# A hand-written order for the first four chunks of a recurrent-attention and two-MLP kernel

## Chip, core and metric

The kernel runs on one core of a Trainium2 chip. The metric is the device time of one execution in microseconds (us); below, the time is that of the profiled execution or the median of several, as said. Engines are named as in the profile: PE (TensorE, matmuls), PEld (its weight loads), DVE (VectorE), ACT (ScalarE), POOL (GpSimd), SP (SyncE, whose queue issues all DMAs here).

## What is computed

A recurrent state update per batch and head, whose output goes through a dense MLP, whose output goes through a layer of eight weighted experts:

```
B, H, S, D = 4, 8, 768, 40
for t in range(S):
    y[:, :, t] = einsum('bhd,bhde->bhe', r_t, state)
    Sa = einsum('bhde,bhe->bhd', state, a_t)
    state = state * w_t[:, :, None, :] - einsum('bhd,bhe->bhde', Sa, b_t) + einsum('bhd,bhe->bhde', v_t, k_t)
x = y as (3072, 320)
h = x @ w_in                                  # 320 x 2048
x = where(h > 0, h, exp(min(h, 0)) - 1) @ w_out
P = exp(x @ w_gate - max); 8 times: rows and columns normalised
out = sum over 8 experts e of P[:, e:e+1] * (relu(x @ w1[e]) @ w2[e])
```

`w_in` and `w_out` arrive as 64-bit floats.

## The kernel before

**Recurrence.** The 768 steps are cut into 24 chunks of 32. `loadw`, `loadk`, `loadv` and `loads2` load a chunk's w and a (`WA`), k and b (`KE`), v (`VU`) and r. `prep` (L308) makes the running products with two scans on DVE (`F` L318, `xE` L324), scales a (`aE`) and copies it to `aB`, and scales `KE` on POOL. `E3` multiplies a against k and b and masks the product on DVE into `Am`; the lower half goes through DRAM (`Ad`), and `LT` loads it back in the layout of the triangular solve. `tsolve` (L401) solves one or two chunks: 31 steps of a product (L416) and a difference (L423) on DVE, and then stores (`Td`) and loads (`TT`) through DRAM. From here the chunks are serial: `H1`, `H2` (needs `TT`, matmuls L462), `H3` and `YW` carry the state from chunk to chunk; `O1` to `O3b` make the chunk's output.

**First MLP.** A block is 256 tokens, two chunks; 12 blocks. `xprep` turns a block's output into `X`. A block is 16 units, one for each 128 columns of `w_in`: eight matmuls L587 into `ph`, two ACT instructions `m`, `g` on DVE (L596), a split into `gh` (ACT) and `gl` (POOL), and two units later eight matmuls L614 to L618. Fp32 products are made from split halves.

**Conversion.** `w_in` and `w_out` stand in SBUF as split fp32, in 32 tiles (16 each). A tile is a load into `raw` (two buffers), an absolute value on ACT (L196), four integer instructions on DVE (L197 to L200, `to_f32`), one copy on ACT and two differences on POOL. A unit n needs the tiles of `w_in` up to n and of `w_out` up to n-2 (`ready`).

**Second MLP.** `phase_b`: per expert, block of 512 tokens and 128 columns, eight matmuls L772, `hh` (ACT), `hl` (DVE), and twelve matmuls L812 to L814.

**What sets the order.** `PLAN["start"]` is a list of tokens for chunks 0 and 1, all conversion (`w_n`: n tiles) and some of chunks 2 to 5. From chunk 2, `PLAN["order"]` is run once for each chunk c: a token `n+o` advances step n of chunk c+o, `m` advances the first MLP by half a unit, `p` advances the solve (three instructions), `G` lets the solve begin, `x` and `xl` advance `xprep`. The scheduler places the instructions of the start and of chunks 2 and 3 by its own model, moved by `issue_after` and `high_priority`. From chunk 4 (`"fixed": 4`) `pin_since` ties every instruction of DVE, ACT, POOL and PE to the one before it in the program, so that the engines run in the written order; SP is not tied. In chunks 2 to 4 only three of four `m` count (`acc`):

```
acc += 3 if c < 5 else 4
if acc >= 4:
    next(mg)
    acc -= 4
```

Of the kernel before, what the change touches and what calls it, by code (L numbers as in the profile page):

```python
# [30 lines left out]
    "fixed": 4,  # L31
    "eng": {"RH": "AA", "VU": "AAAA", "YW": "G", "SS": "AA", "UE": "AV", "XT": "A", "KB": "AA", "AB": "AA"},
# [66 lines left out]
def build(ctx, tc, r, k, v, w, a, b, w_in, w_out, wg, w1, w2, wa_d, kb_d, re_d, ro_d, vt_d, wp_d, consts, out, C, off):  # L99
# [14 lines left out]
    PINNED = {x.engine for x in (V, A, G, T)}  # L114
# [77 lines left out]
    dve = {}  # L192

    def to_f32(raw, tmp):
        lo, hi, m = raw[:, :, 0], raw[:, :, 1], tmp.bitcast(I32)
        A.activation(out=tmp, in_=hi.bitcast(F32), func=AF.Abs)  # L196
# [3 lines left out]
        dve["w"] = V.scalar_tensor_tensor(out=m, in0=lo, scalar=29, in1=m, op0=ALU.logical_shift_right, op1=ALU.bitwise_or)  # L200
        return tmp

    def conv_tiles(n):
        raw = cv.tile([128, n * e32], I32 if wide else F32, tag="raw", name="raw").rearrange("p (f e) -> p f e", e=e32)
        return raw, cv.tile([128, n], F32, tag="tmp", name="tmp", bufs=2) if wide else None

    def w_in_split(cx, n):
        raw, tmp = conv_tiles(3 * n)
        raw = raw.rearrange("p (k f) e -> p k f e", k=3)
        SY.dma_start(out=raw.rearrange("p k f e -> p (k f e)"), in_=wp_d[cx])  # L210
        rf = raw.rearrange("p k f e -> p (k f) e")
        x = (to_f32(rf, tmp) if wide else rf[:, :, 0]).rearrange("p (k f) -> p k f", k=3)
        dl = slice(cx * n, (cx + 1) * n)
        A.activation(out=Wt[:, 0:3, dl], in_=x, func=AF.Copy)
        G.tensor_tensor(out=Wt[:, 3:5, dl], in0=x[:, 0:2, :], in1=Wt[:, 0:2, dl].bitcast(F32), op=ALU.subtract)
        G.tensor_tensor(out=Wt[64:128, 2, dl], in0=x[64:128, 2, :], in1=Wt[64:128, 2, dl].bitcast(F32), op=ALU.subtract)

    def w_out_split(f):
        raw, tmp = conv_tiles(DM)
        SY.dma_start(out=raw.rearrange("p f e -> p (f e)"), in_=wo_d[f * 128:(f + 1) * 128, :])  # L220
        x = to_f32(raw, tmp) if wide else raw[:, :, 0]
        A.activation(out=Wo(f)[:, 0:320], in_=x, func=AF.Copy)
        G.tensor_tensor(out=Wo(f)[:, 320:384], in0=x[:, 256:320], in1=Wo(f)[:, 256:320].bitcast(F32), op=ALU.subtract)
# [84 lines left out]
    def prep(c):  # L308
# [17 lines left out]
        G.tensor_tensor(out=z.aE[0:HR].rearrange("p g t -> p (g t)"), in0=z.WA[0:HR, 1].rearrange("p g t -> p (g t)"), in1=flat(z.xE)[0:HR], op=ALU.mult)  # L326
# [74 lines left out]
    def tsolve(*cs):  # L401
        n = len(cs)
        x0 = cs[0] % 3
        LT2 = LTs[:, x0:x0 + n] if x0 + n <= 3 else LTs[:, ::-2]
        Wk = WkT
        tmp = r1.tile([128, 2 * CI * (C - 1)], F32, tag="Tt", name="Tt")
        w0 = 0 if n == 2 else cs[0] % 2
        Wk = Wk[:, w0:w0 + n]
        SY.dma_start(out=Wk.rearrange("p x i t -> p x (i t)"), in_=consts[:, nidk:nidk + CI * C].unsqueeze(1).to_broadcast([128, n, CI * C]))
        yield  # L410
        for j in range(C - 1):
# [97 lines left out]
    def O1(c):  # L509
# [499 lines left out]
    with ExitStack():  # L1009
        loads(0)  # L1010
# [20 lines left out]
        def ready(n):  # L1031
# [3 lines left out]
            if not wgen:  # L1035
                return True
# [25 lines left out]
        def step(n, c):  # L1062
            if 0 <= c < NCH and (n, c) not in done:
                po = PLAN["po"].get(n, 0)
                with tc.high_priority(offset=po) if po else ExitStack():
                    run_all(fns[n](c) or ())
                done.add((n, c))

# [11 lines left out]
        def solve(n):  # L1080
            for _ in range(n):
                if pump and next(pump[0], "end") == "end":
                    pump.pop(0)
                    pumping.pop()

        def conv(n):
            for _ in range(n):
                if wgen:
                    fn, *ar = wgen.pop(0)
                    cvd.add(("i" if fn is w_in_split else "o", ar[0]))  # L1090
                    with tc.issue_after(dve["A"].ins) if "A" in dve else ExitStack():
                        fn(*ar)
                    if not wgen:
                        cvx.close()
                        late.append(moe.enter_context(tc.tile_pool(name="late", bufs=1)))

        order = [(t.split("+")[0], int((t + "+0").split("+")[1])) for t in PLAN["order"].split()]
        with ExitStack():
            rec_init()
            for t in PLAN["start"].split():  # L1100
                n, *cs = t.split("_")
                cs = [int(x) for x in cs]
                if n == "w":
                    conv(*cs)
                elif n == "xl":
                    xgen.append(xprep(0))
                    run_all(xgen.pop())
                    ms["xp"] = 1
                elif n == "T":
                    with tc.issue_after(dve["w"].ins) if "w" in dve else ExitStack():  # L1110
                        run_all(tsolve(*cs))
                    dve["A"] = dve["T"]
                    done.update(("T", x) for x in cs)
                elif n == "u":
                    advance("T", cs[0])
                elif n == "t":
                    with tc.high_priority(offset=PLAN["po"]["T"]):
# [74 lines left out]
```

## Time and profile before

| What | us |
|---|---|
| median of three runs (2338.56 to 2345.97) | 2342.83 |
| the profiled execution's own time | 2343.14 |
| its span | 2341.0 |
| PE busy in it | 2169.7 |
| DVE busy | 988.0 |
| ACT busy | 752.7 |
| POOL busy | 472.2 |

The span is the time between the first and the last recorded instruction; 2.1 us of the execution lie outside it. Busy times of the engines overlap one another. A line such as "251.35 0.28 PE L462 MATMUL P<-RH,TT ... x2 [1.25 <-DMA TT<-Td]" reads: at 251.35 us from the start, 0.28 us long, line 462 of the kernel, output and inputs by the program's names, two instructions, and the engine had been idle for 1.25 us until a DMA into TT from Td landed.

### The profile page before, as it was taken

Reading aid. Unit: us, or ns where it says so; the run is one execution under the profiler, and the core shown is the slowest. Engines: PE = TensorE matmul, PEld = TensorE weight load, DVE = VectorE, ACT = ScalarE, POOL = GpSimd, SP = SyncE. Lnnn points to the kernel's source line nnn. Section 1 sums busy time; section 2 is a strip of 40 time slices with the busy share of each in tenths; the row PEclk is TensorE's granted clock in tenths of the full one; section 3 lists DMA queues with packets and bytes.
Section 4 is the critical chain, followed back from the end, with each engine's and each line's share of the span. In section 5 each row is a group of like instructions: output and inputs, shape, how many; then the busy total and the mean of one; then the engine's idle time right before and its main releaser. Section 6 shows DMA issues by size and latency. Waiting matters only on the chain.

```text
span 2341.0 us, 47093 instructions
## 1 busy us (share of the span) xinstructions
PE 2169.7 (93%) x19908; PEld 1968.5 (84%) x19908; DVE 988.0 (42%) x2112; ACT 752.7 (32%) x1663; POOL 472.2 (20%) x556
## 2 busy tenths in 40 slices
PE   2377899999999999999999999999999999999998
PEld 2266788888888998888988988988988988988887
DVE  6788666677777522532222222222222222222222
ACT  3243354555555556323212112112112112112111
POOL 5254244343343226002002002002002002001000
PEclk9987799999999999999999999999999999999999
DMA  5344333343333223101001001001001001000000
GB/s 158 99 141 112 92 94 97 102 108 96 100 91 101 64 57 104 60 1 41 10 1 45 6 1 45 6 1 45 6 1 47 4 1 47 4 1 20 23 23 25
DMA packets 171589, 121.62 MB, mean 52 GB/s; under 512 B 102825, under 2 KB 151337, under 8 KB 171369
## 3 DMA queue, kind: packets, MB, share of 16 engines
q1 hardware_dynamic: 171368, 118.52, 18.8%
q8 instruction: 158, 2.59, 0.5%
q14 instruction: 63, 0.51, 0.1%
HBM read 99.99 MB, written 18.48 MB: 51 GB/s over the span
## 4 chain that ended last, share of the span: by engine, by line
PE 73%; DVE 11%; DMA 8%; SPq 3%; ACT 2%; issue 2%; POOL 1%; DVEq 0%; ACTq 0%; POOLq 0%
PE h L772 30%; PE pa L812 9%; PE pa L813 9%; PE pa L814 9%; PE ph L587 4%; DVE Wk L423 3%; DVE Tt L416 2%; DMA LT<-Ad 2%; PE a L614 2%; DMA WA<-in_wa 1%; DMA Ad<-Am 1%; PE a L616 1%; PE a L615 1%; DMA raw<-in_wp 1%; PE P L544 1%
## 5 line engine op out<-in xcount | busy, mean ns | idle before, releaser
L772 PE MATMUL h<-X,a 128*128 128x512 f32 x3072 | 782.0, 396 | 0.6 <-DVE X L575 0.6
L772 PEld LDWEIGHTS h<-X,a 128*128 128x128 f32 x3072 | 564.1, 188 | 107.4 <-DVE X L575 0.8
L776 DVE SCALAR_TENSOR_TENSOR hl<-h,hh 128x512 fp32r<-128x512 f32 x384 | 264.9, 690 | 884.1 <-ACT hh L775 884.0
L775 ACT ACTIVATE hh<-h 128x512 fp32r<-128x512 f32 x384 | 229.3, 598 | 1030.5 <-PE h L772 1022.6
L813 PE MATMUL pa<-a,hl 128*128 128x320 f32 x1536 | 475.1, 310 | 0.0
L812 PE MATMUL pa<-a,hh 128*128 128x320 f32 x1536 | 473.7, 310 | 0.3 <-ACT logits L642 0.3
L814 PE MATMUL pa<-a,hh 128*128 128x320 f32 x1536 | 469.3, 310 | 0.0
L813 PEld LDWEIGHTS pa<-a,hl 128*128 128x128 f32 x1536 | 289.3, 188 | 17.9
L812 PEld LDWEIGHTS pa<-a,hh 128*128 128x128 f32 x1536 | 289.8, 189 | 15.3 <-ACT logits L642 0.4
L814 PEld LDWEIGHTS pa<-a,hh 128*128 128x128 f32 x1536 | 287.4, 188 | 0.0
L740 POOL TENSOR_TENSOR a<-rw,a 128x384 fp32r<-128x384 f32 x64 | 65.2, 1018 | 1062.9 <-ACT a L738 1059.5
L600 POOL TENSOR_TENSOR gl<-g,gh 128x256 fp32r<-128x256 f32 x192 | 165.0, 859 | 396.3 <-ACT gh L598 305.5
L587 PE MATMUL ph<-X,Wt 128*128 128x256 f32 x1536 | 237.3, 299 | 6.1 <-DVE g L596 6.1
L587 PEld LDWEIGHTS ph<-X,Wt 128*128 128x128 f32 x1536 | 206.3, 199 | 11.3 <-DVE g L596 7.3
L423 DVE TENSOR_TENSOR Wk<-Wk,Tt 128x120 f32<-128x120 f32 (+30 forms) x403 | 158.1, 392 | 9.3 <-DVE Tt L416 0.2
L596 DVE SCALAR_TENSOR_TENSOR g<-m,ph 128x256 f32<-128x256 f32 x192 | 80.0, 417 | 167.4 <-ACT m L590 143.3
L416 DVE TENSOR_TENSOR Tt<-Wk,LT 128x120 f32<-128x120 f32 (+30 forms) x403 | 130.8, 324 | 37.0 <-DMA LT<-Ad 12.9
L823 DVE SCALAR_TENSOR_TENSOR acc<-pa,Pg,acc 128x320 f32<-128x320 f32 x168 | 84.3, 544 | 116.0 <-PE pa L814 116.0
L598 ACT ACTIVATE gh<-g 128x256 fp32r<-128x256 f32 x192 | 80.0, 417 | 144.5 <-DVE g L596 143.5
L589 ACT ACTIVATE m<-ph 128x256 f32<-128x256 f32 x192 | 73.2, 381 | 142.2 <-PE ph L587 135.0
L590 ACT ACTIVATE m<-m 128x256 f32<-128x256 f32 x192 | 80.0, 417 | 5.7
L614 PE MATMUL a<-gh,WoB 128*128 128x256 f32 x216 | 71.0, 329 | 1.2 <-ACT gh L598 1.2
(168 smaller groups left out, 2295.7 us busy)
## 6 DMA issues: line engine op xcount, KB each, us to landing
LT<-Ad SPq DMA_DIRECT2D x24, 512.0 KB
rw<-in_moe_w SPq DMA_DIRECT2D x64, 160.0 KB
WA<-in_wa SPq DMA_DIRECT2D x24, 416.0 KB
KE<-in_kb SPq DMA_DIRECT2D x24, 416.0 KB
rw<-in_moe_w SPq DMA_DIRECT2D x64, 128.0 KB
VU<-in_vt SPq DMA_DIRECT2D x24, 320.0 KB
raw<-in_wp SPq DMA_DIRECT2D x16, 384.0 KB
raw<-in_moe_w_out SPq DMA_DIRECT2D x16, 320.0 KB
```

What stands on the lines that cost most here:

```text
L416: V.tensor_tensor(out=tv, in0=Wk[:, :, 0:ni, j:j + 1].to_broadcast(sh), in1=LT2[:, :, j, j + 1:C].unsqueeze(2).to_broadcast(sh), op=ALU.mult,)
L423: dve["T"] = V.tensor_tensor(out=Wk[:, :, 0:ni, j + 1:C], in0=Wk[:, :, 0:ni, j + 1:C], in1=tv, op=ALU.subtract)
L587: T.matmul(ph, lhsT=Wt[0:kp, wi, 128 * f:128 * f + 128], rhs=X[0:kp, xi, :], start=(i == 0), stop=(i == 7))
L600: G.tensor_tensor(out=gl, in0=g, in1=gh.bitcast(F32), op=ALU.subtract)
L614: T.matmul(o, lhsT=Wo(f)[:, 128 * i:128 * i + 128], rhs=gh, start=(s and i == 0), stop=False, skip_group_check=True)
L772: T.matmul(h, lhsT=a1[:, wi, :], rhs=X[bk][:, xi, :], start=(i == 0), stop=(i == 7))
L775: A.activation(out=hh, in_=h, func=AF.Relu)
L776: V.scalar_tensor_tensor(out=hl, in0=h, scalar=0.0, in1=hh.bitcast(F32), op0=ALU.max, op1=ALU.subtract)
L812: T.matmul(o, lhsT=hh[:, ts_], rhs=a2[:, 0, :], start=(f == 0), stop=False)
L813: T.matmul(o, lhsT=hl[:, ts_], rhs=a2[:, 0, :], start=False, stop=False)
L814: T.matmul(o, lhsT=hh[:, ts_], rhs=a2[:, 1, :], start=False, stop=(f == NF2 - 1))
L823: V.scalar_tensor_tensor(out=at, in0=o, scalar=Pg[:, tt, e:e + 1], in1=at, op0=ALU.mult, op1=ALU.add)
```

## The change

The four parts of it, cut to their core (the steps themselves are those above):

- The start and the lists of chunks 2 and 3 (`"first"`) are written out and pinned on all engines and on SP's queue. `prep_0*5` stands for five tokens, `s_n` for n steps of a solve. In chunks 2 and 3 every `m` counts.
- Conversion goes one tile per `p`, 4 tiles' steps in the start (`w`) and the rest in chunks 2 and 3; the steps of neighbouring tiles are staggered (`conv`).
- Chunks 2 and 3 are solved as one pair, with their factors in the memory of chunk 1's `WA` and `KE` (`two`) and their unknowns in that of chunk 1's `wq`.
- Solve 4/5 follows the conversion, 16 instructions per `p`. `aE` of chunks 0 and 1 is made on DVE, `E1` of chunks 0 and 1 uses other PSUM banks, and `uE` of chunks below 4 is copied on ACT.

```diff
-    PINNED = {x.engine for x in (V, A, G, T)}
+    PINNED = {x.engine for x in (V, A, G, T, SY)}
-            if x.engine in PINNED:
+            if x.engine in PINNED and (queue or x.engine != SY.engine):
...
+        def conv_begin():
+            convs.extend(conv_load(*wlist[i]) for i in range(2))
+            conv_abs(convs[0])
...
+        def conv():
+            k = cvn[0]
+            if k > NW:
+                return False
+            if k:
+                conv_out(convs[k - 1])
+            if k + 1 < NW:
+                conv_abs(convs[k + 1])
+            if k < NW:
+                conv_bits(convs[k])
+            if k + 2 < NW:
+                convs.append(conv_load(*wlist[k + 2]))
...
+    def lt(c):
+        return two[:, c - 2].rearrange("p (s t) -> p s t", s=C) if c in (2, 3) else LTs[:, c % 3]
...
+        LT2 = two.rearrange("p x (s t) -> p x s t", s=C) if cs[0] == 2 else LTs[:, x0:x0 + n] if x0 + n <= 3 else LTs[:, ::-2]
+        Wk = work[1][1].rearrange("p (x i) t -> p x i t", x=2) if cs[0] == 2 else WkT
...
-                if n == "w":
-                    conv(PLAN["wn"])
-                elif n == "m":
-                    acc += 3 if c < 5 else 4
-                    if acc >= 4:
-                        next(mg)
-                        acc -= 4
+                if n == "m":
+                    next(mg)
                 elif n == "p":
-                    if pumping:
-                        pk += 1
-                        solve(PLAN["tp"][c % 2][pk % 2])
+                    if c >= 4 or not conv():
+                        if pumping:
+                            solve(PLAN["tp"][c % 2] if c >= 4 else PLAN["tp1"])
...
-                if c >= PLAN["fixed"]:
-                    pin_since(last)
+                pin_since(last, c < 4)
```

What it does to the order is seen in three places. First DVE while the second solve runs: before, the single solve of chunk 2 (`Tt`, `Wk`) alternates with the four conversion instructions of a tile (`tmp`).

```order
L200 SCALAR_TENSOR_TENSOR tmp<-raw,tmp 128x320
L416 TENSOR_TENSOR Tt<-Wk,LT 128x69
L423 TENSOR_TENSOR Wk<-Wk,Tt 128x3x23
L197 TENSOR_SCALAR tmp<-tmp 128x384
L416 TENSOR_TENSOR Tt<-Wk,LT 128x66
L198 TENSOR_SCALAR tmp<-tmp 128x384
L423 TENSOR_TENSOR Wk<-Wk,Tt 128x3x22
L199 SCALAR_TENSOR_TENSOR tmp<-raw,tmp 128x384
```

With the change, DVE at the end of chunk 3: the last tile's four instructions, a unit's `g`, the output of chunk 3 (`xT`), and only then solve 4/5.

```order
L200 TENSOR_SCALAR tmp<-tmp 128x320
L201 TENSOR_SCALAR tmp<-tmp 128x320
L202 SCALAR_TENSOR_TENSOR tmp<-raw,tmp 128x320
L203 SCALAR_TENSOR_TENSOR tmp<-raw,tmp 128x320
L625 SCALAR_TENSOR_TENSOR g<-m,ph 128x256
L576 TENSOR_TENSOR xT<-P_101,xT 128x160
L576 TENSOR_TENSOR xT<-P_102,xT 128x160
L444 TENSOR_TENSOR Tt<-Wk,LT 128x62
L451 TENSOR_TENSOR Wk<-Wk,Tt 128x2x31
L444 TENSOR_TENSOR Tt<-Wk,LT 128x60
```

No tile of the conversion is left behind this place, and no solve stands between the tiles of chunks 2 and 3. Second, SP's queue with the change, where solve 2/3 ends (`Td` from `wq`): the stores and loads of both chunks come in a row, and the next `raw` load waits behind them.

```order
L218 DMA raw<-in_moe_w_out 128x640
L456 DMA Td<-wq_143 256x1x32 x8
L462 DMA TT_109<-Td 32x8x32 x4
L462 DMA TT_110<-Td 32x8x32 x4
L218 DMA raw<-in_wp 128x768
L437 DMA Wk<-in_consts 128x2x256
L331 DMA rB<-in_re 40x8x64 x2
L333 DMA rO<-in_ro 104x512
L218 DMA raw<-in_moe_w_out 128x640
L218 DMA raw<-in_wp 128x768
```

Before, the two chunks are solved apart, and single `raw` loads stand between the stores and loads of each. Third, PE around `H2` of chunk 6 (L491 with the change): from the last unit ahead of it to the next, no matmul of the first MLP stands here.

```order
L429 MATMUL P_99<-VU,Am_116 64x40 x8
L429 MATMUL P_100<-VU,Am_116 64x40 x8
L393 MATMUL P_102<-aB,KE 64x64 x16
L479 MATMUL P_99<-Yw,aE 32x40 x16
L479 MATMUL P_100<-Yw,aE 32x40 x16
L384 MATMUL P_101<-cst,xE 128x104 x4
L491 MATMUL P_100<-RH,TT_109 64x40 x16
L375 MATMUL P_101<-cst,KE 128x104 x4
L375 MATMUL P_102<-cst,KE 128x104 x4
L599 MATMUL P_102<-cst,yt 128x128 x3
L514 MATMUL P_99<-VU,KB 40x40 x16
```

Before, each of these steps has a half of a unit beside it. Counted on PE ahead of `H2` of chunks 4, 5, 6 and 7, there are 14, 20, 28 and 36 units (L587) before, and 18, 26, 32 and 36 (L616) with the change; from chunk 7 on the two orders of PE agree.

## Rows read from the trace of the kernel before

**Rows 1.** Windows: us, busy per engine (with counts), granted PE clock, DMA share, GB/s.
```profile
93.80:162.00 68.20, 47.19 (x713) 39.49 (x713) 56.49 (x157) 30.02 (x69) 30.13 (x44) 0.96 0.48 141
162.00:251.30 89.30, 67.27 (x933) 59.09 (x929) 72.58 (x183) 31.54 (x81) 36.23 (x41) 0.68 0.41 105
251.30:350.80 99.50, 89.32 (x1518) 83.44 (x1518) 68.54 (x158) 50.42 (x126) 36.18 (x42) 0.93 0.39 99
...
417.70:871.50 453.80, 426.30 (x7369) 399.04 (x7368) 289.01 (x683) 243.37 (x617) 166.11 (x197) 0.98 0.35 89
871.50:2341.00 1469.50, 1455.72 (x8144) 1312.57 (x8140) 393.66 (x695) 333.91 (x626) 140.61 (x157) 1.00 0.08 23
```

**Rows 2.** Timeline of PE: `H2` of chunks 0, 1, 4, 5, 6, 7.
```profile
88.99 0.41 PE L462 MATMUL P<-RH,TT 64*64 64x40 f32 x2 [18.28 <-DMA TT<-Td]
...
113.42 2.00 PE L462 MATMUL P<-RH,TT 64*64 64x40 f32 x32 [0.50 <-ACT RH L438]
...
251.35 0.28 PE L462 MATMUL P<-RH,TT 64*64 64x40 f32 x2 [1.25 <-DMA TT<-Td]
...
285.80 1.13 PE L462 MATMUL P<-RH,TT 64*64 64x40 f32 x32
316.91 1.13 PE L462 MATMUL P<-RH,TT 64*64 64x40 f32 x32
350.78 1.13 PE L462 MATMUL P<-RH,TT 64*64 64x40 f32 x32
```

**Rows 3.** Timeline of DVE: first and last step of solves 0/1 and 4/5.
```profile
51.72 0.16 DVE L416 TENSOR_TENSOR Tt<-Wk,LT 128x62 f32<-128x62 f32 x1
...
81.78 0.18 DVE L423 TENSOR_TENSOR Wk<-Wk,Tt 128x16 f32<-128x16 f32 x1
...
219.68 0.22 DVE L416 TENSOR_TENSOR Tt<-Wk,LT 128x62 f32<-128x62 f32 x1 [6.33 <-DMA Ad<-Am]
...
242.85 0.18 DVE L423 TENSOR_TENSOR Wk<-Wk,Tt 128x16 f32<-128x16 f32 x1
```

**Rows 4.** The chain that ended last, in order of time: start, us, what.
```profile
42.40 7.18 DMA WA<-in_wa
...
452.32 3.86 DMA Ad<-Am
456.19 4.56 DMA LT<-Ad
```

**Rows 5.** Timeline of ACT: absolute values of tiles 1, 8 and 27 of 32.
```profile
13.33 0.55 ACT L196 ACTIVATE tmp<-raw 128x384 f32<-128x384 f32 x1 [1.22 <-DMA raw<-in_wp]
...
93.85 0.56 ACT L196 ACTIVATE tmp<-raw 128x384 f32<-128x384 f32 x1
...
162.01 0.48 ACT L196 ACTIVATE tmp<-raw 128x320 f32<-128x320 f32 x1
```

**Rows 6.** Groups by line: a tile's four DVE instructions; busy us, mean ns, idle before.
```profile
L199 DVE SCALAR_TENSOR_TENSOR tmp<-raw,tmp 128x384 int32<-128x384 int32 (+1 forms) x32 | 20.3, 638 | 0.2
...
L200 DVE SCALAR_TENSOR_TENSOR tmp<-raw,tmp 128x384 int32<-128x384 int32 (+1 forms) x32 | 19.3, 604 | 0.2
...
L197 DVE TENSOR_SCALAR tmp<-tmp 128x384 f32<-128x384 f32 (+1 forms) x32 | 15.2, 478 | 14.5 <-ACT tmp L196 14.4
...
L198 DVE TENSOR_SCALAR tmp<-tmp 128x384 int32<-128x384 int32 (+1 forms) x32 | 14.3, 449 | 0.3
```

**Rows 7.** Timeline of DVE: one step of solve 0/1 beside a product on POOL.
```profile
60.27 0.30 DVE L423 TENSOR_TENSOR Wk<-Wk,Tt 128x132 f32<-128x132 f32 x1
60.60 1.15 DVE L416 TENSOR_TENSOR Tt<-Wk,LT 128x126 f32<-128x126 f32 x1
```

**Rows 8.** Timeline of POOL at that time.
```profile
60.36 2.42 POOL L335 TENSOR_TENSOR KE<-KE,F 104x512 f32<-104x512 f32 x2 [2.43 <-DMA KE<-in_kb]
```

**Rows 9.** Timeline of PE: the first half of a unit, twice.
```profile
144.44 2.07 PE L587 MATMUL ph<-X,Wt 128*128 128x256 f32 x8
...
340.09 1.22 PE L587 MATMUL ph<-X,Wt 128*128 128x256 f32 x8
```

More of the change, by code (lines that the diff above doesn't have):

```diff
@@ L118, in traced, with pin_since @@
         return nc.cur_bb.bb.instructions
-    def pin_since(last):
+    def pin_since(last, queue):
         ins = traced()
-        k = next(k for k in reversed(range(len(ins))) if ins[k] is last) + 1
+        k = next(k for k in reversed(range(len(ins))) if ins[k] is last) + 1 if last is not None else 0
         for x in ins[k:]:
-            if x.engine in PINNED:
+            if x.engine in PINNED and (queue or x.engine != SY.engine):
                 if x.engine in pins:
@@ new lines, in to_f32, with conv_load @@
+    def to_f32(raw, tmp):
+        f32_abs(raw, tmp)
+        f32_bits(raw, tmp)
+        return tmp
+    convs = []
+    cvd = set()
+    def conv_load(kind, i):
+        z = K()
+        z.kind, z.i = kind, i
+        n = 384 if kind == "i" else DM
+        z.raw = cv.tile([128, n * e32], I32 if wide else F32, tag="raw", name="raw")
+        SY.dma_start(out=z.raw, in_=wp_d[i] if kind == "i" else wo_d[i * 128:(i + 1) * 128, :])
+        z.rv = z.raw.rearrange("p (f e) -> p f e", e=e32)
+        z.n = n
+        return z
@@ new lines, in conv_abs, with conv_bits, conv_out @@
+    def conv_abs(z):
+        if wide:
+            z.x = cv.tile([128, z.n], F32, tag="tmp", name="tmp")
+            f32_abs(z.rv, z.x)
+        else:
+            z.x = z.rv[:, :, 0]
+    def conv_bits(z):
+        if wide:
+            f32_bits(z.rv, z.x)
+    def conv_out(z):
+        if z.kind == "i":
+            x = z.x.rearrange("p (k f) -> p k f", k=3)
+            dl = slice(z.i * 128, z.i * 128 + 128)
+            A.activation(out=Wt[:, 0:3, dl], in_=x, func=AF.Copy)
+            G.tensor_tensor(out=Wt[:, 3:5, dl], in0=x[:, 0:2, :], in1=Wt[:, 0:2, dl].bitcast(F32), op=ALU.subtract)
+            G.tensor_tensor(out=Wt[64:128, 2, dl], in0=x[64:128, 2, :], in1=Wt[64:128, 2, dl].bitcast(F32), op=ALU.subtract)
+        else:
+            f, x = z.i, z.x
+            A.activation(out=Wo(f)[:, 0:320], in_=x, func=AF.Copy)
+            G.tensor_tensor(out=Wo(f)[:, 320:384], in0=x[:, 256:320], in1=Wo(f)[:, 256:320].bitcast(F32), op=ALU.subtract)
+            G.tensor_tensor(out=Wo(f)[:, 384:640], in0=x[:, 0:256], in1=Wo(f)[:, 0:256].bitcast(F32), op=ALU.subtract)
+        cvd.add((z.kind, z.i))
@@ L255, in build @@
     work = {None: (wr, wq, dq, aB)}
+    two = sp.tile([128, 2, C * C], F32, name="two")
     def rec_init():
@@ L265, in rec_init @@
             V.memset(bank[i], 0.0)
-        for t in (aB, wmm, rB, *TTs, Yw):
+        work[1] = (early(1, "wr", [4 * NG, C + 1]), early(1, "wq", [4 * NG, C]), early(1, "dq", [4 * NG, C]), early(1, "aB", [NG * 2 * 2, 64]).rearrange("p (g u j) t -> p g u j t", u=2, j=2))
+        for t in (aB, wmm, *work[1]):
             G.memset(t, 0.0)
@@ L269, in rec_init, with rec_init2 @@
         G.memset(whalf, 1e-5 - (WHI - WLO) / 2)
+    def rec_init2():
         for i in (0, 1):
             V.memset(bank[i], 0.0)
+        for t in (rB, *TTs, Yw):
+            G.memset(t, 0.0)
     def flat(t):
@@ L1009, in build @@
     with ExitStack():
+        first_ins = traced()[-1] if traced() else None
         loads(0)
@@ L1051, in build @@
         mg = msteps()
-        cvd = set()
-        wi_ = [(w_in_split, i, 128) for i in range(NF1)]
-        wo_ = [(w_out_split, i) for i in range(NF1)]
         k0 = PLAN["lead"]
-        wgen = wi_[:k0]
+        wlist = [("i", i) for i in range(k0)]
         for i in range(NF1):
-            wgen += wi_[k0 + i:k0 + i + 1] + wo_[i:i + 1]
+            wlist += [("i", k0 + i)] * (k0 + i < NF1) + [("o", i)]
+        NW = len(wlist)
         fns = dict(ld=loads, ldw=loadw, ldk=loadk, lu=loadv, lv=loads2, prep=prep, H1=H1, H2=H2, H3=H3, H4=H4, E1=E1, E2=E2, E3=E3, E4=E4, T=tsolve, O1=O1, O2=O2, O3a=O3a, O3b=O3b, YW=YW, LT=LT)
         done = {("ld", 0), ("ld", 1)}
[L1062 to L1067, printed above, removed]
         going = {}
@@ L1083, in solve @@
                     pump.pop(0)
[L1084 to L1102, printed above, removed]
-                if n == "w":
[L1104 to L1117, printed above, removed]
-                        run_all(going[("T", cs[0])])
-                    done.add(("T", cs[0]))
-                else:
-                    step(n, cs[0])
@@ L1122, in build @@
-        acc = pk = 0
+                    if pumping:
+                        pumping.pop()
+        def conv_begin():
+            convs.extend(conv_load(*wlist[i]) for i in range(2))
+            conv_abs(convs[0])
+        cvn = [0]
+        def conv():
[10 more added lines that the diff above has]
+                convs.append(conv_load(*wlist[k + 2]))
+            if k == NW:
+                cvx.close()
+                late.append(moe.enter_context(tc.tile_pool(name="late", bufs=1)))
+            cvn[0] += 1
+            return True
@@ new lines, in tokens @@
+        def tokens(x):
+            out = []
+            for t in x.split():
+                t, k = (t + "*1").split("*")[:2]
+                out += [t] * int(k)
+            return out
+        rec_init()
+        pin_since(first_ins, True)
+        for t in tokens(PLAN["start"]):
+            last = traced()[-1]
+            n, *cs = t.split("_")
+            cs = [int(x) for x in cs]
+            if n == "cl":
+                conv_begin()
+            elif n == "w":
+                conv()
+            elif n == "z":
+                rec_init2()
+            elif n == "xl":
+                xgen.append(xprep(0))
+                run_all(xgen.pop())
+                ms["xp"] = 1
+            elif n == "u":
+                pump.append(tsolve(*(cs if len(cs) == 2 else (cs[0], cs[0] + 1))))
+                next(pump[-1])
+            elif n == "s":
+                had = len(pump)
+                for _ in range(cs[0]):
+                    if len(pump) == had:
+                        solve(1)
+            else:
+                advance(n, cs[0])
+            pin_since(last, True)
@@ L1123, in build @@
+        acc = 0
         for c in range(2, NCH + 1):
-            for n, o in order:
+            for t in tokens(PLAN["first"][c - 2] if c < 4 else PLAN["order"]):
+                n, o = (t.split("+") + ["0"])[:2]
+                o = int(o)
                 last = traced()[-1]
-                if n == "w":
-                    conv(PLAN["wn"])
-                elif n == "m":
-                    acc += 3 if c < 5 else 4
-                    if acc >= 4:
-                        next(mg)
-                        acc -= 4
+                if n == "m":
+                    next(mg)
@@ L1143, in build @@
                     if c % 2 == 0 and c + 3 < NCH:
+                        while pump:
+                            solve(1)
                         pump.append(tsolve(c + 2, c + 3))
```

68 lines of the change are left out of this document (24 added, 44 removed), and 10 rows, old and new, of the table PLAN.

## Prediction

> **What bounds the kernel now.** I first read the windows [rows 1]. From 871.5 us to the end PE is busy 1455.7 of 1469.5 us: the second MLP is bound by PE, and the change does not touch it. From 417.7 to 871.5, the chunks in their fixed order, PE is busy 94%. From 93.8 to 251.3 it is busy 114.5 of 157.5 us, at a granted clock that falls to 0.68 in the second part. What can be won lies there and ahead of it, where PE waits for the recurrence and the conversion. DVE has the most work in that part: 56.5 of 68.2 us, 83%, from 93.8 to 162.
>
> Next I looked for a mark behind which both programs are the same. That is `H2` of chunk 7 [rows 2]: at 350.78 us, and by the order both programs have put 36 units of the first MLP on PE ahead of it, and the same sequence behind it. So the time with the change is 2343.1 us, the profiled execution's own (0.3 above the median of the runs), less what this mark moves forward. The six units by which the change is ahead at chunk 5 (26 against 20) are no gain by themselves: block 2 needs the output of chunk 5, so the lead is used up in chunk 6, where the order shows no units. What stays is only the mark's place in time.
>
> **The parts of the change, in order of time.**
>
> *Up to the first solve.* Before, solve 0/1 begins at 51.72 [rows 3], behind five tiles of conversion and four preparations. With the change only three preparations and two tiles precede it, and ACT's queue begins with the first tile's absolute value, which has its data at 13.33 [rows 5]; the copies of `aB` stand behind it, about 15 us. WA of chunk 2 goes into chunk 0's buffer, whose last reader is ACT, at about 17; such a load takes 7.2 [rows 4], the preparation and the mask product some 3, and `Ad` and `LT` 3.9 + 4.6 [rows 4]. 17 + 7.2 + 3 + 8.4 = 35.6: I take 36. Bounds: 30, if the load takes half of it, and 52, if nothing is won.
>
> *Solve 0/1.* Before it takes 30.2 us (51.72 to 81.96) with two waits for WA; solve 4/5, with less beside it, takes 23.3 (219.68 to 243.03) [rows 3]. Between them, as one preparation and two mask products lie inside: 28, so it ends at 64.
>
> *Chunks 0 and 1.* From the end of solve 0/1 to `H2` of chunk 0 it was 7.0 us (81.96 to 88.99) [rows 2, 3]: 71. From there the order binds solve 2/3 to the serial chain of both chunks: DVE has no other work, and can't run ahead of the waits for `Y`, `Gm` and `xT`. Before, `H2` of chunk 1 came 24.4 us behind that of chunk 0 [rows 2], with conversion in between on DVE. A chain of two chunks without it I put at 35 (an estimate: the 24.4 cut to 15 as the tiles go, and 20 for chunk 1 with its output and `xprep`); bounds 30 and 49 (twice 24.4). The end is 106, where the first unit can start.
>
> *Into the conversion.* The sixth tile's load stands on SP behind the 16 stores and loads of solve 2/3, which cost DVE and ACT a wait. From the end of a solve to `H2` behind these DMAs it was 7.0 and 8.3 us (243.03 to 251.35) [rows 2, 3]; then its own load, ACT, four instructions of 2.2 us in all [rows 6], and the seventh tile the same: 18, so the seventh tile leaves DVE at 124. Bounds 12 and 22.
>
> *The tiles.* 25 more tiles follow, each with its share of four preparations, two chunks and 15 units. Before, with the same two buffers, the absolute values of tiles 8 and 27 are 68.2 us apart, 19 steps: **3.59 us a tile** [rows 5]. The loop is the load into a buffer, ACT, DVE, and the load again. I take 3.59: 90 us, to 214. The lower bound is DVE at work all the time: 56.5 us in that stretch for 19 tiles is 2.97. Before, a solve stood between the tiles; now it is preparations and units, about as much. The upper bound comes with the rivals.
>
> *Solve 4/5* now follows the tiles, beside few units: 23.3, to 237. *`H2` of chunk 4* comes 8.3 later [rows 2, 3]: 245.4, against 251.35 before. So the hand-written order wins only 6 us here: the 16 us of the early start are mostly given back, as 28 of 32 tiles and a whole solve now stand in a row behind chunk 1.
>
> *Chunks 4 to 6.* Before, 99.4 us from there to the mark, with 22 units. Now 18 units. A half of a unit is 1.22 us at full clock [rows 9], a whole one 2.44, four of them 9.8. It counts in full where PE is the bound: before, chunk 5 to 6 takes 31.1 us with 8 units [rows 2], and PE is busy 89.3 of 99.5 in the stretch [rows 1]. Chunk 6 will in part be bound by its chain instead; I take 9 (bounds 0 and 14, with the slower clock at its start won as well): 90.4, to 335.8.
>
> The mark moves from 350.8 to 335.8, and the sum is 2343.1 - 15.0 = **2328 us**. With a cadence of c us a tile it is 2328 + 25 (c - 3.59).
>
> What I cost at nothing: `aE` of two chunks on DVE instead of POOL, which DVE hides in its wait for WA; the clearing of banks moved behind the first preparation, in the same wait; other PSUM banks for `E1`; the copy of `uE` on ACT. If DVE does not wait there, they cost about 3 us. SP, now tied too, has in chunks 2 and 3 a wait for `Ad` ahead of each `LT`, with tiles' loads behind it: up to 3.9 us [rows 4], three times, and I count it in the 3.59, in whose stretch of the trace such waits fall as well.
>
> A rule and a row. A step of the solve that takes 0.30 us takes 1.15 while POOL multiplies in SBUF [rows 7, 8]. The Trainium skill, page "SBUF — State Buffer", section "Who interferes with whom", says that a DVE instruction with two SBUF inputs contends with a GpSimd instruction that reads SBUF, and that the later one blocks until the other is done; the trace agrees with it (0.30 against 1.15 us). By this rule the change is to lose, since it puts the differences of a tile on POOL and the next tile's two-input instructions on DVE at the same time, unit after unit; that is the second rival.
>
> **The rivals.**
>
> *DVE sets the pace of the tiles* (chance 0.23). If the staggered steps hide load and ACT, c is 2.97 and the time 2328 - 15.5 = 2312. For it: each absolute value is issued a whole tile ahead. Against it: with two buffers a load can't start before DVE has left the buffer.
>
> *POOL blocks DVE* (0.18). If each tile loses one half of a blocked step, 0.43 us, DVE's work is 3.40 a tile, and at the 83% of before c is 4.10: 2341, no change. For it: POOL was busy 30.1 of 68.2 us [rows 1] and now has units all along. Against: the 3.59 and the means of rows 6 hold some of this already.
>
> *PE stays at half clock through chunks 2 and 3* (0.10), the slower side. Half a unit took 2.07 us at 144 against 1.22 at 340 [rows 9], though the profile gives a clock of 1.0 for the early part, and between 162 and 251 the clock was 0.68 with PE busy 75% [rows 1]. The lower level is 1.2 GHz. At it a unit is 4.1 us, and a chunk's other matmuls (31.1 less eight units is 11.6 at full clock) up to 23, 2.9 a unit: 7.0 a unit, 3.5 a tile if PE never waits, 4.7 at 75%. That gives 2356, slower; the point from which it decides is a cadence of 4.5. The Trainium skill, page "TensorE: Matmul & The Clock Gate", Part 1, says that the throttled state is the default and that activity releases it; no run here shows yet how these two chunks will fare.
>
> *The early start does not come* (0.05): the queue is now bound, and a late load holds all behind it. With the first solve at 52 the time is 2344, the same as before.
>
> **How the numbers follow.** The forecast, a cadence near 3.6, has 0.42, and by itself 2318 to 2338. About 0.3% (7 us) is what a measurement of this kernel can tell from no change. Faster: most of 0.42, all of 0.23 and a little of the second rival, 0.62. Same: 0.25. Slower: 0.13, the third rival and the bounds that add up (a chain of 49 instead of 35). The range for 8 in 10 reaches from 2304, the first rival with the early bounds, to 2350, past the second rival and short of the third.
>
> **What would show it.** In the profile of the changed kernel: the first solve step at 33 to 40 us; `H2` of chunk 0 near 71; the first unit near 106; 25 tiles at 3.3 to 3.9 us; solve 4/5 alone for 23 us, beginning near 214; `H2` of chunk 4 near 245 and of chunk 7 near 336; no units around `H2` of chunk 6; and from the mark to the end of the span the 1990 us of before (2341.0 - 350.8). I am wrong if the distance from the mark to the end differs by more than 5 us, if the cadence lies outside 3.2 to 4.2, or if PE is the engine that the tiles wait for.

## The result and the profile after

The changed kernel takes 2360.35 us (median of four runs, 2353.38 to 2363.02) against 2340.69 for the kernel before beside it: ratio 1.0076, 95% interval 1.0052 to 1.0100. It is slower, by 0.8%; I had forecast 2328, with 2350 as the upper end. The profiled execution takes 2363.02 us, with a span of 2361.2.

Windows of the changed kernel, cut at the points of the forecast (columns as in [rows 1]): `H2` of chunk 0, the seventh tile leaving DVE, the last tile leaving DVE, `H2` of chunks 4 and 7, the end.

```profile
0.00:74.18 74.18, 17.68 (x208) 15.25 (x209) 59.65 (x129) 18.89 (x39) 22.57 (x32) 0.68 0.55 146
74.18:124.23 50.05, 29.12 (x660) 25.89 (x662) 36.20 (x77) 15.96 (x37) 14.82 (x19) 0.64 0.27 65
124.23:236.60 112.37, 70.96 (x871) 66.04 (x869) 83.65 (x139) 53.22 (x127) 50.89 (x74) 0.65 0.48 137
236.60:270.76 34.16, 17.82 (x201) 16.36 (x200) 24.36 (x72) 9.90 (x25) 7.25 (x12) 0.63 0.13 29
270.76:373.51 102.75, 91.58 (x1458) 84.76 (x1458) 66.21 (x158) 45.27 (x111) 33.83 (x39) 0.78 0.39 102
373.51:2361.20 1987.69, 1938.70 (x16519) 1765.23 (x16518) 718.05 (x1477) 611.83 (x1328) 328.41 (x380) 0.99 0.15 41
```

The third and the fifth row hold the loss. The 25 tiles take 112.37 us where I had 90, **4.49 us a tile**; chunks 4 to 6 take 102.75 where I had 90.4. The other points stand in the timeline of DVE (solve 0/1, tiles 7 and 32, solve 4/5; before: [rows 3, 5]) and of PE (`H2`, now L491; before: [rows 2]).

```profile
33.77 0.22 DVE L444 TENSOR_TENSOR Tt<-Wk,LT 128x62 f32<-128x62 f32 x1 [1.11 <-DMA LT<-Ad]
...
65.51 0.19 DVE L451 TENSOR_TENSOR Wk<-Wk,Tt 128x16 f32<-128x16 f32 x1
...
122.87 1.36 DVE L203 SCALAR_TENSOR_TENSOR tmp<-raw,tmp 128x320 int32<-128x320 int32 x1
...
236.11 0.49 DVE L203 SCALAR_TENSOR_TENSOR tmp<-raw,tmp 128x320 int32<-128x320 int32 x1
...
237.31 0.24 DVE L444 TENSOR_TENSOR Tt<-Wk,LT 128x62 f32<-128x62 f32 x1
...
261.92 0.19 DVE L451 TENSOR_TENSOR Wk<-Wk,Tt 128x16 f32<-128x16 f32 x1
```

```profile
74.18 0.40 PE L491 MATMUL P<-RH,TT 64*64 64x40 f32 x2 [13.41 <-DMA TT<-Td]
...
270.76 0.28 PE L491 MATMUL P<-RH,TT 64*64 64x40 f32 x2 [1.62 <-DMA TT<-Td]
...
373.51 1.13 PE L491 MATMUL P<-RH,TT 64*64 64x40 f32 x32
```

What DVE does in the 25 tiles: groups by line of the four instructions of a tile (busy us, mean ns, idle before; the shapes 320 and 384 mixed), and who waits for whom.

```profile
L203 DVE SCALAR_TENSOR_TENSOR tmp<-raw,tmp 128x320 int32<-128x320 int32 (+1 forms) x25 | 18.3, 732 | 0.9
L200 DVE TENSOR_SCALAR tmp<-tmp 128x320 f32<-128x320 f32 (+1 forms) x25 | 16.3, 650 | 23.2 <-ACT tmp L196 23.2
L202 DVE SCALAR_TENSOR_TENSOR tmp<-raw,tmp 128x320 int32<-128x320 int32 (+1 forms) x25 | 16.0, 639 | 0.9
L201 DVE TENSOR_SCALAR tmp<-tmp 128x320 int32<-128x320 int32 (+1 forms) x25 | 10.0, 401 | 0.9
```

```profile
DVE tmp L200 <- ACT tmp L196: 23.2, 15, 3.0
ACT tmp L196 <- POOL Wt L240: 19.1, 10, 2.1
...
ACT tmp L196 <- DMA raw<-in_moe_w_out: 9.7, 4, 2.6
...
ACT tmp L196 <- POOL WoB L245: 8.6, 6, 1.9
...
ACT tmp L196 <- DMA raw<-in_wp: 5.4, 1, 5.4
...
ACT tmp L196 <- POOL WoA L245: 3.7, 3, 1.4
```

In the stretch of before from which I took 3.59, DVE was busy 56.5 of 68.2 us for 19 tiles [rows 1], 2.97 a tile, and idle 0.62. Now it is busy 83.65 / 25 = 3.35 and idle 1.15. So 0.37 of the 0.90 more is busy time and 0.53 idle time. Most of the idle time (23.2 of 28.7 us) is a wait for ACT's absolute value, and this waits 31.4 us (19.1 + 8.6 + 3.7) for POOL and 15.1 for loads: by the written order `conv_out(k-1)` stands ahead of `conv_abs(k+1)` on ACT, `tmp` has two buffers, and the new absolute value needs the one that POOL's differences of tile k-1 still read. In the pinned order ACT does nothing else meanwhile. The busy time is longer by blocking, as this timeline of DVE and POOL shows:

```profile
155.36 1.28 POOL L353 TENSOR_TENSOR aE<-WA,xE 104x512 f32<-104x512 f32 x1 [3.05 <-DVE xE L351]
155.51 2.69 DVE L200 TENSOR_SCALAR tmp<-tmp 128x320 f32<-128x320 f32 x1
...
156.60 0.73 POOL L629 TENSOR_TENSOR gl<-g,gh 128x256 fp32r<-128x256 f32 x1
...
157.29 0.73 POOL L239 TENSOR_TENSOR Wt<-tmp,Wt 128x256 fp32r<-128x256 f32 x1
```

An instruction that takes 0.33 us with POOL idle takes 2.69 here.

### The profile page after: what moved, and what is told of

The parts are those of the page before. It is cut to its first block, busy times and chain, and to the rows that moved or that the text cites. A ratio compares the mean times of both kernels' runs of the same rounds, so it can differ in the third digit from the quotient of the medians.

```text
span 2361.2 us, 47101 instructions
## 1 busy us (share of the span) xinstructions
PE 2165.9 (92%) x19908; PEld 1973.5 (84%) x19908; DVE 988.1 (42%) x2048; ACT 755.1 (32%) x1667; POOL 457.8 (19%) x554
## 4 chain that ended last, share of the span: by engine, by line
PE 74%; DVE 7%; DMA 3%; SPq 3%; ACT 1%; issue 1%; POOL 0%; DVEq 0%; POOLq 0%; ACTq 0%
PE h L801 30%; PE pa L842 10%; PE pa L841 10%; PE pa L843 10%; PE ph L616 5%; DVE Tt L444 2%; DVE Wk L451 1%; SPq L456 1%; PE a L643 1%; PE P L393 1%; PE a L644 1%; PE a L645 1%; SPq L462 1%; DVE g L625 1%; PE pg L669 1%
## 5 line engine op out<-in xcount | busy, mean ns | idle before, releaser
L616 PE MATMUL ph<-X,Wt 128*128 128x256 f32 x1536 | 247.1, 307 | 9.0 <-DVE g L625 6.9
L629 POOL TENSOR_TENSOR gl<-g,gh 128x256 fp32r<-128x256 f32 x192 | 151.9, 791 | 435.1 <-ACT gh L627 329.8
L616 PEld LDWEIGHTS ph<-X,Wt 128*128 128x128 f32 x1536 | 212.5, 205 | 16.7 <-DVE g L625 8.3
L451 DVE TENSOR_TENSOR Wk<-Wk,Tt 128x120 f32<-128x120 f32 (+24 forms) x341 | 126.0, 369 | 10.6 <-DVE Tt L444 0.4
L444 DVE TENSOR_TENSOR Tt<-Wk,LT 128x120 f32<-128x120 f32 (+24 forms) x341 | 119.7, 351 | 16.9 <-DMA LT<-Ad 8.6
L393 PE MATMUL P<-aB,KE 104*64 104x64 f32 x736 | 32.2, 253 | 50.3 <-POOL KE L362 27.6
```

The source lines that it names most:

```text
L444: V.tensor_tensor(out=tv, in0=Wk[:, :, 0:ni, j:j + 1].to_broadcast(sh), in1=LT2[:, :, j, j + 1:C].unsqueeze(2).to_broadcast(sh), op=ALU.mult,)
L616: T.matmul(ph, lhsT=Wt[0:kp, wi, 128 * f:128 * f + 128], rhs=X[0:kp, xi, :], start=(i == 0), stop=(i == 7))
L629: G.tensor_tensor(out=gl, in0=g, in1=gh.bitcast(F32), op=ALU.subtract)
```

## Experiments

Theory: the written order closes a loop DVE, ACT, POOL, ACT through the two `tmp` buffers (and another through the two of `raw`), and what is left is DVE blocked by POOL. Rivals: PE at half clock paces the tiles; POOL's blocking alone; the units' chain. The cadence is the time per tile of the last 25 tiles, from the seventh tile leaving DVE to the last, as above. Where a run was executed once, its marks are read and not its time: from `H2` of chunk 7 to the end the written order is the same (but for e7, whose units come later), and yet the profiled executions took from 1980.5 us (e1) to 1997.9 (e4) for it.

**e1: a third `tmp` buffer.**

```diff
-            z.x = cv.tile([128, z.n], F32, tag="tmp", name="tmp")
+            z.x = cv.tile([128, z.n], F32, tag="tmp", name="tmp", bufs=3)
-        tmp = r1.tile([128, 2 * CI * (C - 1)], F32, tag="Tt", name="Tt")
+        tmp = r1.tile([128, 160], F32, tag="Tt", name="Tt")
```

> In the changed kernel the last 25 tiles leave DVE 4.49 us apart (124.2 to 236.6 us). In that stretch DVE waits 23.2 us for ACT's absolute values, and these wait 31.4 us in all for POOL's differences of the tile two places earlier, whose tmp buffer they need, and 15.1 us for loads. Here tmp has a third buffer (Tt is cut to the 160 elements that it uses, to make room); the order of all engines is the same. Theory (the tmp buffer loop ACT, POOL, ACT, DVE sets the pace): ACT no longer waits for POOL, DVE's wait falls by 23.2 x 31.4 / 46.5 = 15.7 us, the cadence to 3.7 to 4.0, H2 of chunk 4 comes near 255 us instead of 270.8, the time is near 2345. Rival 1 (PE at half clock paces the tiles): the cadence stays at 4.4 to 4.6 and the time within 3 us of the changed kernel. Rival 2 (POOL blocks DVE in SBUF): DVE's busy time per tile stays at 3.35 us or grows, the cadence stays above 4.2.

Cadence 4.34, `H2` of chunk 4 at 270.5, ratio to before 1.0063 (1.0044 to 1.0081). The theory's number failed, and the time isn't clear of the changed kernel's. The waits show why:

```profile
ACT tmp L196 <- DMA raw<-in_moe_w_out: 18.0, 10, 3.9
...
DVE tmp L200 <- ACT tmp L196: 11.6, 11, 3.4
...
ACT tmp L196 <- DMA raw<-in_wp: 10.9, 4, 7.7
...
ACT tmp L196 <- POOL Wt L239: 1.4, 1, 1.4
```

The wait for POOL is gone but for 1.4 us, that for loads has nearly doubled to 28.9, and the integer instructions grew from 60.6 to 66.4 us.

**e2: half of the units' matmuls.**

```diff
-        for i, (wi, xi, kp) in enumerate(ORD1):
+        ords = ORD1 if blk else ORD1[:4]
+        for i, (wi, xi, kp) in enumerate(ords):
...
+            if not blk:
+                continue
```

> Leaves out half of the matmuls of the units of block 0 (low parts of the products), which run in chunks 2 and 3; nothing else changes in the order. Rival 1 (PE at half clock paces the tiles): the units' matmuls are some 55 of the 71 us that PE is busy between 124.2 and 236.6 us, so the 25 tiles get shorter by 20 to 27 us and the cadence falls to 3.4 to 3.7. Theory (buffer loop) and rival 2 (POOL blocks DVE): PE only has more idle time, the cadence stays at 4.3 to 4.5 and H2 of chunk 4 within 5 us of 270.8.

Cadence 4.58, `H2` of chunk 4 at 271.0. The window of the 25 tiles, columns as above:

```profile
122.26:236.70 114.44, 59.65 (x780) 53.30 (x776) 83.43 (x139) 53.09 (x127) 50.67 (x74) 0.60 0.48 135
```

PE is busy 59.65 us instead of 70.96 (less is saved than I had said: without any units, in e7, it is still busy 40.03 us), and nothing comes of it: the units' matmuls don't pace the tiles, at a clock of 0.60. DVE itself waits for PE only 0.4 us there, as in the changed kernel.

**e3: no differences on POOL.**

```diff
-        G.tensor_tensor(out=Wt[:, 3:5, dl], ...)
-        G.tensor_tensor(out=Wt[64:128, 2, dl], ...)
+        if z.i == 4:
+            G.memset(Wt[:, 3:5, 512:2048].bitcast(F32), 0.0)
...
```

The first four tiles of `w_in` keep their differences; for `w_out` the edit is alike, with two more clears.

> Leaves out POOL's differences of 28 tiles (the low halves of the weights stay zero, cleared three times in the conversion). The tmp buffer is then free after ACT's copy, and POOL does not read tmp or the weights. Theory: ACT's 31.4 us of waits for POOL are gone, DVE's wait falls by about 16 us, and of the 18.6 us by which the integer instructions in the 25 tiles are longer than their shortest forms some 10 go as well: cadence 3.3 to 3.6, H2 of chunk 4 near 245. If it falls below e1 by more than 0.3 us a tile, blocking by POOL (rival 2) has its own share. Rival 1 (PE at half clock): cadence 4.3 to 4.6.

Cadence 4.14, missed again, and only 0.20 under e1, less than the 0.3 that would have been a sign of blocking: ACT's wait for POOL is gone, that for loads is 25.6 us, and DVE still waits 16.5 us for ACT.

**e4: three of four `m`.**

```diff
                 if n == "m":
-                    next(mg)
+                    acc += 3 if c < 5 else 4
+                    if acc >= 4:
+                        next(mg)
+                        acc -= 4
```

> Only three of four m count again in chunks 2 to 4, as in the kernel before, so that by the order 14, 20, 28 and 36 units stand ahead of H2 of chunks 4, 5, 6 and 7 instead of 18, 26, 32 and 36. Theory for chunks 4 to 6 (102.75 us against the 90.4 of the forecast): the lead runs out in chunk 6, where 26 us have no unit and the chain runs at half clock, so units moved there from chunks 2 to 4 cost next to nothing: H2 of chunk 4 to H2 of chunk 7 takes 97 to 104 us although it holds four more units, PE's granted clock in chunk 6 is above 0.9, the part ahead of H2 of chunk 4 gets 2 to 6 us shorter, the time is 2352 to 2358. Rival (a unit costs its 2.44 us wherever it stands): the stretch takes 110 to 115 us, the time is 2360 or more.

The changed kernel counts every `m` in chunk 4 too, so the edit reaches chunks 2 to 4. Ratio 1.0036 (1.0015 to 1.0057), median 2354.2 us. `H2` of chunk 4 comes at 263.9, that of chunk 7 at 356.8: **92.9 us for 22 units, against 102.75 for 18**, less than the 97 that I had as the least. Chunk by chunk it is 29.7, 29.5 and 33.8 us against 33.2, 28.0 and 41.6, and 34.5, 31.1 and 33.9 in the kernel before: the loss is in chunk 6. From `H2` of chunk 6 to that of chunk 7, first in the changed kernel, then here:

```profile
331.95:373.51 41.56, 32.71 (x463) 29.22 (x462) 24.56 (x59) 14.75 (x35) 9.34 (x11) 0.63 0.40 110
```

```profile
323.02:356.79 33.77, 30.27 (x528) 28.24 (x527) 25.72 (x62) 19.21 (x48) 13.65 (x16) 1.00 0.48 130
```

PE is busy nearly as long in both, with more matmuls here: the granted clock is 1.00 instead of 0.63. In the changed kernel no unit stands between the first and the last of these rows of PE, 26 us:

```profile
328.49 0.28 PE L647 MATMUL a<-gl,WoB 128*128 128x256 f32 x1
...
334.27 1.93 PE L491 MATMUL P<-RH,TT 64*64 64x40 f32 x30 [2.02 <-DMA TT<-Td]
...
355.29 2.07 PE L616 MATMUL ph<-X,Wt 128*128 128x256 f32 x8
```

Each of the chain's own matmuls is slower there. One group of 64, in the changed kernel and then here:

```profile
339.95 2.13 PE L514 MATMUL P<-VU,KB 64*40 64x40 f32 x64
```

```profile
329.50 1.30 PE L514 MATMUL P<-VU,KB 64*40 64x40 f32 x64
```

Added up from this `H2` to the last group ahead of the next unit (L562), the same groups take 15.1 us and 8.7, and the two chunks' times are 7.8 us apart. A wait of 2.0 us for `TT`, seen above, comes on top in the changed kernel.

The time shows less of this: the mark comes 16.7 us earlier than in the changed kernel, the profiled execution is only 6.6 us shorter, as the part behind the mark takes 1997.9 us here. Why that part is longer isn't shown.

**e5 and e6: three buffers for `raw` too; with e4's `m`.**

```diff
+        if cvk[0] >= 6 and cvk[0] % 3 == 2:
+            z.raw = LTi[:, 0].rearrange("p s t -> p (s t)")[:, 0:n * e32]
...
-            if k + 2 < NW:
-                convs.append(conv_load(*wlist[k + 2]))
+            for j in ([k + 2] if k < 5 else [7, 8] if k == 5 else [k + 3]):
+                if j < NW:
+                    convs.append(conv_load(*wlist[j]))
```

> With the third tmp buffer (e1) the cadence of the last 25 tiles was 4.33 us, not 3.7 to 4.0: ACT's 31.4 us of waits for POOL went, but its waits for loads into raw rose from 15.1 to 28.9 us, and the integer instructions on DVE from 2.43 to 2.66 us a tile (1.75 undisturbed). Here raw has a third buffer as well from the sixth tile on (in the memory of LT 0, whose load for chunk 6 moves behind the last tile), and a load is issued three tiles ahead. If the loads were the next limit: ACT's waits for raw fall below 8 us, DVE's 11.6 us of waits for ACT nearly vanish, cadence 3.85 to 4.05, H2 of chunk 4 at 258 to 265, time 2345 to 2351. If POOL in SBUF is the limit under all buffers (rival 2): the integer instructions grow beyond 2.8 us a tile and the cadence stays above 4.2.

e5: cadence 3.91, `H2` of chunk 4 at 256.9, 2347.7 us, ratio 1.0030 (1.0006 to 1.0055). The window of the 25 tiles and DVE's remaining wait:

```profile
125.37:223.06 97.69, 62.02 (x877) 57.72 (x874) 91.37 (x139) 52.57 (x127) 53.74 (x76) 0.75 0.53 149
```

```profile
DVE tmp L200 <- ACT tmp L196: 1.3, 3, 0.7
```

DVE is now busy 94%. The tiles' own instructions take 71.4 us, 2.86 a tile, the most of all runs. So one of rival 2's two signs came (above 2.8 us a tile), the other didn't (a cadence above 4.2).

> e5 with the three of four m of e4 in chunks 2 to 4. If both gains add: the cadence 0.1 to 0.2 us under e5's, H2 of chunk 4 to H2 of chunk 7 at 93 to 100 us with 22 units as in e4 (92.9), H2 of chunk 7 at 347 to 352, time 2339 to 2345: level with the kernel before. If the limit is POOL and DVE alone (rival 2), it stays at e4's 2354.

e6: cadence 3.91, `H2` of chunk 4 at 253.2 and of chunk 7 at 347.2 (94.0 between them), 2334.8 us, ratio 0.9965 (0.9949 to 0.9981): a little faster than the kernel before. Both repairs add, though not by the cadence, which I had expected 0.1 to 0.2 below e5's.

**e7: no units in chunks 2 and 3; e8: these chunks not pinned.**

```diff
                 if n == "m":
-                    next(mg)
+                    if c > 3:
+                        next(mg)
```

```diff
-                pin_since(last, c < 4)
+                if c >= 4:
+                    pin_since(last, False)
```

> No m counts in chunks 2 and 3, so that the 25 tiles have no units of the first MLP beside them (two buffers each, as in the changed kernel); the units come later, so only the part up to H2 of chunk 4 compares. Theory U: my 3.59 came from a stretch with 3 instructions g in 19 tiles, the changed kernel has 13 in 25 tiles, and every unit passes through PE, ACT, DVE, ACT and POOL in queues that can't be passed: without them the cadence is 3.3 to 3.8 and H2 of chunk 4 at 248 to 255. Rival T (the tile's own loop through ACT and POOL and the preparations set it): the cadence stays above 4.1. PE at half clock (rival 1) was answered by e2 already: half of the matmuls left out, cadence 4.58.

e7: cadence 4.01, between the two; `H2` of chunk 4 at 256.0. With two buffers each, the units cost some 0.5 us a tile, but DVE still waits 20.1 us for ACT.

> The start stays pinned, chunks 2 and 3 are not: the scheduler may move their instructions on all engines and on SP's queue, as in the kernel before. Theory (waits in written order carry over from engine to engine): the cadence falls to 3.5 to 4.0 and H2 of chunk 4 comes at 245 to 260. Rival: the tiles are limited by resources (DVE with POOL in SBUF, buffers), the cadence stays at 4.2 to 4.6.

e8: the cadence is 4.34, but doesn't compare, because solve 4/5 now begins at 162 and runs between the tiles. `H2` of chunk 4 comes at 255.5, 15 us earlier; one time, 2339.1 us.

**e9, e10: the parts of e5.** e9 has e5's `raw` and the old `tmp`; e10 only the move of `LT+3`.

> e5 without the third tmp buffer: raw has three, tmp two. In e5 the cadence fell to 3.91 us and DVE's idle time between the tiles to almost nothing. If the waits stand behind one another and both buffers are needed, ACT still waits some 30 us for POOL here and the cadence is 4.2 to 4.5. If raw was the limit all along (e1 gave only 0.16 us a tile), it is 3.9 to 4.0.

> Control for e5: only the load LT of chunk 6 moves behind the last tile, all buffers as in the changed kernel. Expected: cadence 4.4 to 4.55, time within 4 us of the changed kernel's. If this load on SP's queue was a part of e5's gain, the cadence is below 4.3.

e9: 4.29, with no wait for loads left and 40.2 us of waits for POOL; e10: 4.53, so the place of that load on SP's queue is no part of e5's gain. Against e10 the third `raw` alone gives 0.24 us a tile, the third `tmp` alone 0.16 (e1 against the changed kernel), both together 0.6: the waits stand behind one another.

**e11: e5 with e3's edit.**

> e5 and leaves out POOL's differences of 28 tiles as e3 did. In e5 DVE has no idle time left between the tiles, and the integer instructions take 2.85 us a tile, 1.75 undisturbed. Theory (the last layer is DVE blocked by POOL in SBUF): they fall to 2.0 to 2.3 us a tile and the cadence to 3.1 to 3.4. Rival (they are long for another reason, such as the loads that write SBUF): they stay above 2.6 and the cadence above 3.7.

Cadence 3.65, integer instructions 2.42 us a tile: between theory and rival, so each instruction is taken by itself. I call excess what an instruction takes beyond the shortest of its form (0.33, 0.35, 0.49, 0.56 us). In e11 34 of 100 instructions overlap a POOL instruction, with 17.6 us of excess, and 66 don't, with 0.1. In e5 it is 28.5 against 0.0, in the changed kernel 17.6 against 0.1. So the excess comes with POOL and not with the loads, whose DMA share was 0.59 in these tiles of e11. Leaving out the differences left `gl`, `aE`, `KE` and my clears to block:

```profile
170.53 2.50 POOL L253 MEMSET WoB<- 128x2880 f32 x1
...
170.67 2.57 DVE L200 TENSOR_SCALAR tmp<-tmp 128x384 f32<-128x384 f32 x1 [1.21 <-ACT tmp L196]
```

**e12: e6 with chunks 2 and 3 not pinned.**

> e6 (three tmp, three raw, three of four m) with chunks 2 and 3 left to the scheduler as in e8, whose single time was 2339 and whose H2 of chunk 4 came at 255.5, as solve 4/5 ran between the tiles. If the gains add: H2 of chunk 4 at 240 to 248, time 2322 to 2331, faster than the kernel before and than e6 (2334.8). If DVE's work is the limit in both, the order matters no more: H2 of chunk 4 at 249 to 256, time 2331 to 2338.

2319.96 us, ratio **0.9904** (0.9886 to 0.9921): faster than both kernels. Timeline of DVE: solve 4/5 begins between the tiles and ends 4 us behind the last; PE has `H2` of chunk 4 at 241.2 and of chunk 7 at 334.9.

```profile
168.32 0.47 DVE L450 TENSOR_TENSOR Tt<-Wk,LT 128x62 f32<-128x62 f32 x1 [0.65 <-DMA LT<-Ad]
...
227.91 0.60 DVE L203 SCALAR_TENSOR_TENSOR tmp<-raw,tmp 128x320 int32<-128x320 int32 x1
...
232.21 0.19 DVE L457 TENSOR_TENSOR Wk<-Wk,Tt 128x16 f32<-128x16 f32 x1
```

```profile
241.18 0.28 PE L497 MATMUL P<-RH,TT 64*64 64x40 f32 x2 [0.18 <-DMA TT<-Td]
...
334.91 1.13 PE L497 MATMUL P<-RH,TT 64*64 64x40 f32 x32
```

In e6 the last tile leaves DVE at 220.5, and the solve alone follows: 12 us later in all. Which of the scheduler's moves are needed for this beside that of the solve wasn't tried.

## Why the prediction was wrong

*The frame held.* The mark moved, and from it to the end it is 1987.7 us against the 1990 I had (that it is so near is in part luck: the other runs lie between 1980.5 and 1997.9, e7 left aside). It only moved the other way: 373.5 instead of 335.8.

*Up to the seventh tile the steps held*, though the trace of before shows none of this order: first solve 33.8 (36), its end 65.7 (64), `H2` of chunk 0 at 74.2 (71), the seventh tile 124.2 (124). The early start is real. Between these points errors cancel: from `H2` of chunk 0 to the first unit it is 29.6 us where I had 35, and from there to the seventh tile 20.4 where I had 18.

*"I take 3.59" for the tiles is the step that failed most*: 112.4 us instead of 90, 22.4 of the 37.7. I had written that a loop of load, ACT, DVE and load sets it. The loop through POOL, by which a `tmp` buffer comes free, was missing: in the kernel before, ACT's order was the scheduler's, and in those 19 tiles ACT waited 0.6 us for POOL and 23.9 for loads, DVE 8.0 for ACT. Who waits for whom there, in the kernel before:

```profile
ACT tmp L196 <- DMA raw<-in_moe_w_out: 13.1, 8, 2.5
ACT tmp L196 <- DMA raw<-in_wp: 10.8, 7, 2.7
DVE tmp L197 <- ACT tmp L196: 8.0, 11, 1.2
...
ACT tmp L196 <- POOL WoA L224: 0.6, 1, 0.6
```

The code showed it, as `conv_out(k-1)` stands directly ahead of `conv_abs(k+1)`. And "preparations and units, about as much" as a solve counted DVE's work, not what a unit does to the others: 13 units pass in the 25 tiles, 3 in the 19 of before, each with its subtraction on POOL and its turn on ACT. e1, e5 and e9 show the two buffer loops, e7 the units' share, e5 and e11 the blocking under them. With both loops open DVE is the bound, at 3.65 us of work a tile, not 2.97.

The row itself was a favourable one, which I overlooked. In the kernel before, cut where tiles 8, 27 and 32 leave DVE, as 4.49 was measured:

```profile
98.28:170.37 72.09, 50.64 (x709) 42.90 (x706) 61.63 (x165) 31.12 (x71) 36.42 (x49) 0.91 0.46 134
170.37:197.03 26.66, 21.85 (x269) 19.61 (x268) 25.67 (x58) 16.00 (x44) 17.21 (x21) 0.93 0.45 124
```

The same 19 steps are 3.79 us each on DVE, and the last five, with six units beside them (three in the 19), 5.33: 4.11 over all 24. My own sum with 4.11 gives 2341, no change.

*Chunks 4 to 6 are the second*: 12.35 us. I counted four units fewer as 9 us won. Without them PE idles in chunk 6, the chain runs at a granted clock of 0.63, and the stretch is longer than with four units more (e4): chunk 6 takes 41.6 us against 33.9 before, while chunks 4 and 5 do win 4.4. The lead was no gain, as I had said, but it was a loss, which I hadn't.

*Solve 4/5 and the way to `H2` of chunk 4* held: 24.8 and 8.7 us (23.3 and 8.3). That this solve stands alone behind the tiles was known; e12 shows that it need not.

*The rivals.* The slower one, PE at half clock, has nearly the right time (2356), by luck, and the wrong cause: the granted clock is 0.65 in the tiles, but e2 refutes it. Its sum was off as well: it takes half a unit a tile, where the forecast counts 15 units in 25 tiles, and PE's work there is 2.84 us a tile, not 3.5. POOL blocking DVE is right in kind and near in size: the excess is 17.6 us in the 25 tiles, 0.70 each, and counted the same way 6.1 us in the 19 tiles of before (98.28 to 170.37), 0.32 each; that is 0.38 more, where I had 0.43, and DVE's work of 3.35 us a tile is near its 3.40. What it lacked is idle time: 1.15 us a tile, where the 83% of before would leave 0.70. (The chances named add up to 0.98.) The Trainium skill, page "SBUF — State Buffer", section "Who interferes with whom", says besides the rule that I used that tensor_scalar can run in a mode in which it contends with GpSimd as well; the trace agrees, with 2.57 us beside a MEMSET for an instruction of 0.35.

## What to carry to other kernels

When an order is written out and pinned, follow each buffer round its whole loop: who frees it, and what stands on that engine's queue between. A cadence measured in one neighbourhood is not a property of the loop (3.59 here, 4.11 over the last 24 tiles of the same kernel); take it apart into work, waits and blocking, and ask which of them the new neighbours change. Work taken out of a stretch whose chain doesn't depend on it can make the stretch longer, if it kept PE's clock up.

## What the hardware showed

A DVE instruction that waited for POOL wasn't let in between POOL instructions that followed one another: 2.69 us at 155.51, across three of them, and 2.66 to 2.96 us at three more places of the changed kernel. Also, an instruction of POOL that reads nothing (MEMSET, 2.50 us) held a DVE instruction with one input for its whole length (e11). And chunk 6 was shorter with more work in it, as PE's clock stayed up: 33.8 us at 1.00 against 41.6 at 0.63.
